# Cutting a 64-column half block of matmuls into 32-column tiles, next to a stage that already uses them

## The chip, the cores and the metric

The kernel runs on one core of one Trainium2 chip. The metric is the device time of one execution in microseconds (us). A run also has a span, from its first to its last instruction, which is about 1.2 us shorter here. Engines are named as in the profile: PE is the matrix engine (TensorE), PEld its weight loads, ACT is ScalarE, DVE is VectorE, POOL is GpSimd. The granted clock is the share of the full PE clock that the run was given, 1.0 for all of it. "The chain that ended last" is the work followed back from the last instruction, at each step to what released it. L585 means line 585 of the kernel. The change adds two lines, so L585, L661, L674 and L787 of the kernel before are L587, L663, L676 and L789 of the kernel after, and lines move similarly in the experiments.

## The reference, cut to what matters

```python
xn = _layernorm(x)                    # 2048 tokens x 640
s  = _A_ref(xn, wqkv, wo)             # linear attention, 32 heads of 20
h  = max(xn @ w1, 0)                  # w1 is 640 x 1728
g  = silu(h @ w2)                     # w2 is 1728 x 640
return x + s * g
```

The width 1728 is 13 blocks of 128 columns and one half block of 64. The change is about the half block of `xn @ w1`.

## The kernel before

Each full block of `w1` is handled by `H_block`: five matmuls (640 = 5 x 128) of a 128 x 128 stationary operand against 512 tokens, accumulated in one bank of PSUM, the memory that PE writes its sums to. For the half block a 128 x 128 pass would leave half of the array's columns empty. So `H_half` pairs two groups of 512 tokens: one group (u = 0) goes to PSUM partitions 0 to 63, the other (u = 1) to 64 to 127, and the two alternate.

```python
def H_half(jp):
    b = nextb()
    fns = []
    ...
    for k in range(C):                       # C = 5
        for u in range(2):
            src = hsrc(2 * jp + u)[0]
            fns.append(lambda eng, k=k, u=u, src=src: eng.matmul(
                ps[b][64 * u:64 * (u + 1), :], lhsT=w1_sb[:, k, NF * P:FF], rhs=src[:, k, :],
                start=(k == 0), stop=(k == C - 1)))
    a = sc.group("PE", fns, R=[("w1", 2)] + keys, W=[("ps", b)])
    ...   # ACT: relu of the whole bank into hTl
```

The attention's denominators are computed right after it, with 32 columns (one for each head) and four groups of 512 tokens side by side, each at a stated position in the array:

```python
def den():
    ...
    for c in range(C):
        for i in range(J):                   # J = 4
            fns.append(lambda eng, c=c, i=i: eng.matmul(
                ps[b][H * i:H * (i + 1), :], lhsT=zmat[:, c, :], rhs=pqT[:, c, schunk(i)],
                start=(c == 0), stop=(c == C - 1), tile_position=(0, H * i)))
    sc.group("PE", fns, R=[("zmat",)] + [...], W=[("ps", b)])
```

The place of both, late in the first half of the kernel:

```python
if n == 9:
    z_col()                                  # 10 one-column matmuls, L661; DVE makes zmat of them
if n == 11:                                  # after the seventh full block of the last 512 tokens
    lastW1 = H_half(0)
    lastW1 = H_half(1)
    den()
```

The counter n runs over a list that mixes full blocks with other work, so 11 is not a count of full blocks. The six full blocks that are left and then the Gram matmuls (L787, the next stage) follow on PE.

Of the kernel before, what the change touches and what calls it, by code (L numbers as in the profile page):

```python
# [208 lines left out]
def bass_recurrent_scan__linear_attn_block__dense_activation_relu__prompt_kernel(  # L209
# [13 lines left out]
    FF = B_w1.shape[1]  # L223
    P = 128
    T = S // P
    J = S // 512
    C = D // P
    NF = FF // P
# [35 lines left out]
    w1_sb = reg5[:, 0:C * FF].rearrange("p (c n) -> p c n", c=C)  # L264
# [43 lines left out]
    ps = [psT[:, 512 * i:512 * (i + 1)] for i in range(8)]  # L308
# [226 lines left out]
    def nextb():  # L535
        b = RB[ring[0] % len(RB)]
        ring[0] += 1
        return b
# [21 lines left out]
    def hsrc(j):  # L560
        if j == 0:
            return xcT[:, :, :], [("xcT", q, h) for q in range(4) for h in range(2)]
        return xnT[:, :, schunk(j)], [("xnT", 4 * j + q) for q in range(4)]
# [12 lines left out]
# [3 lines that stand above are left out]
        keys = []  # L579
        for u in range(2):  # L580
            keys += hsrc(2 * jp + u)[1]
        for k in range(C):
            for u in range(2):
                src = hsrc(2 * jp + u)[0]
                fns.append(lambda eng, k=k, u=u, src=src: eng.matmul(  # L585
                    ps[b][64 * u:64 * (u + 1), :], lhsT=w1_sb[:, k, NF * P:FF], rhs=src[:, k, :],
                    start=(k == 0), stop=(k == C - 1)))  # L587
        a = sc.group("PE", fns, R=[("w1", 2)] + keys, W=[("ps", b)])
        sc.op("ACT", lambda eng: eng.activation(out=hTl[:, jp, :], in_=ps[b], func=ACTF.Relu),
              R=[("ps", b)], W=[("hTl", jp)])  # L590
        return a
# [129 lines left out]
    for j in range(J):  # L721
        for n, item in enumerate(plans[j]):
# [38 lines left out]
            if j == J - 1:  # L761
                while zpend:
                    z_add()
                if n == 1:
                    z_split()
                if n == 9:
                    z_col()
                if n == 11:
# [3 lines that stand above are left out]
# [232 lines left out]
```

## Time and profile before

| | |
|---|---|
| time | 221.32 us, median of 3 runs (221.1 to 221.34) |
| span of the profiled run | 219.3 us, granted clock 1.0 |
| PE busy | 214.8 us, 98% |
| PE's share of the chain that ended last | 94% |
| half block, L585, in the chain | 20 matmuls, 2.28 us, 1.0% |
| denominators, L674, in the chain | 20 matmuls, 1.19 us, 0.5% |

First the busy table of the kernel before, by engine:

```profile
PE 214.8 (98%) x1431; PEld 133.6 (61%) x1441; DVE 119.0 (54%) x219; ACT 84.2 (38%) x140; POOL 43.7 (20%) x69
```

Then the chain of work that ended last, over the stretch in question (start, length, what). A matmul's piece in this view runs from the end of the one before it to its own end, so pieces add up without overlap. "issue" is time in which the engine waited for nothing that the profile shows.

```profile
98.18 0.23 PE psT L661 x10
98.41 2.18 PE psT L568 x10
100.59 2.28 PE psT L585 x20
102.87 1.19 PE psT L674 x20
104.06 0.16 issue
104.22 6.42 PE psT L568 x29
110.64 21.73 PE psT L787 x160
```

The reader should see that PE works without a break and that twenty half block matmuls take 2.28 us, 114 ns each, while ten full ones (L568) take 2.18 us, 218 ns each. A full one streams the same 512 columns. Only two at a time can do that. The timeline of PE shows the pairs (start, length, line, operands in partitions x columns, count):

```profile
98.27 2.32 PE L568 MATMUL psT<-reg 128*128 128x512 bf16 x10
100.52 0.40 PE L585 MATMUL psT<-regX,reg 128*64 128x512 bf16 x1
100.52 0.40 PE L585 MATMUL psT<-reg 128*64 128x512 bf16 x1
100.76 0.38 PE L585 MATMUL psT<-regX,reg 128*64 128x512 bf16 x1
100.76 0.38 PE L585 MATMUL psT<-reg 128*64 128x512 bf16 x1
...
102.80 1.26 PE L674 MATMUL psT<-pqT,zmat 128*32 128x512 bf16 x20
```

A matmul's length of 0.38 us here is longer than the step to the next one: lengths overlap, and the profiler models their ends. What counts for throughput is the step from start to start. The records behind this view have starts to the nanosecond: within a pair 3 to 4 ns, from pair to pair 215 to 216 ns (241 for the first), and among the denominators 2 to 4 ns within a group of four and 216 ns from group to group (226 for the first). I call such a group that starts together a pass. The half block is ten passes, the denominators five.

### The profile page before, as it was taken

To read this page: it belongs to the slowest core of one execution; us is meant where nothing else is said; L and a number is where in the kernel's file an instruction comes from. 1 tells how busy PE (TensorE), PEld (TensorE's weight loads), DVE (VectorE), ACT (ScalarE), POOL (GpSimd) and SP (SyncE) were. 2 spreads that over 40 slices of the span, in tenths; PEclk is the share of its full clock that TensorE was granted. 3 is DMA by queue.
4 is the path that set the end of the run, shared out by engine and by line. 5 is a ranking of instruction groups with operands and counts; after the bars stand their busy time and mean duration, and the time that the engine had idled before them with its cause. 6 is when DMAs were issued, how large, how long until landed. Compare 5 with 4: busy or idle time off the path is not lost.

```text
span 219.3 us, 3503 instructions
## 1 busy us (share of the span) xinstructions
PE 214.8 (98%) x1431; PEld 133.6 (61%) x1441; DVE 119.0 (54%) x219; ACT 84.2 (38%) x140; POOL 43.7 (20%) x69
## 2 busy tenths in 40 slices
PE   8999999999999999999999999999999999999995
PEld 7655554555545555444467777677767776777674
DVE  3789957779639999783702116930424240403134
ACT  5597675666655676554420000551021102110211
POOL 2178501120041699950000000000000000000001
DMA  6977496711001243000099969942110100001011
GB/s 205 368 234 161 110 302 59 199 30 30 3 1 38 51 107 106 0 0 3 3 209 303 374 215 341 373 132 64 38 52 33 60 30 30 33 30 61 3 60 60
DMA packets 28421, 24.72 MB, mean 113 GB/s; under 512 B 12021, under 2 KB 27765, under 8 KB 28405
## 3 DMA queue, kind: packets, MB, share of 16 engines
q1 hardware_dynamic: 24677, 19.77, 32.1%
q10 hardware_dynamic: 3728, 4.73, 6.4%
q8 instruction: 11, 0.18, 0.4%
q14 instruction: 5, 0.04, 0.1%
HBM read 15.81 MB, written 5.24 MB: 96 GB/s over the span
## 4 chain that ended last, share of the span: by engine, by line
PE 94%; DMA 2%; ACT 1%; DVE 1%; issue 0%; DVEq 0%
PE psT L847 26%; PE psT L568 25%; PE psT L787 10%; PE psT L546 10%; PE psT L493 9%; PE psT L898 9%; DMA reg<-in_A_x_dram 2%; PE psT L865 1%; PE psT L585 1%; PE psT L817 1%; PE psT L802 1%; PE psT L674 1%; DVE reg L886 0%; ACT regE L447 0%; PE psT L468 0%
## 5 line engine op out<-in xcount | busy, mean ns | idle before, releaser
L847 PE MATMUL psT<-reg,hT 128*128 128x320 bf16 x416 | 60.5, 299 | 0.0
L847 PEld LDWEIGHTS psT<-reg,hT 128*128 128x128 bf16 x416 | 40.2, 98 | 16.5 <-issue 1.1
L568 PE MATMUL psT<-reg 128*128 128x512 bf16 x192 | 45.5, 379 | 0.3 <-issue 0.2
L886 DVE TENSOR_TENSOR reg<-psT,reg 128x640 bf16<-128x640 f32 (+2 forms) x18 | 13.3, 749 | 48.3 <-PE psT L898 47.0
L572 ACT ACTIVATE hT<-psT 128x512 bf16<-128x512 f32 x52 | 30.8, 602 | 18.1 <-PE psT L568 18.1
L568 PEld LDWEIGHTS psT<-reg 128*128 128x128 bf16 x195 | 18.9, 98 | 21.9 <-issue 0.4
L875 ACT ACTIVATE reg<-psT 128x640 bf16<-128x640 f32 x12 | 8.2, 701 | 44.7 <-PE psT L847 25.3
L891 POOL TENSOR_TENSOR reg<-reg 128x224 bf16<-128x224 bf16 x1 | 0.6, 607 | 120.4 <-DVE reg L886 120.4
L898 PE MATMUL psT<-reg,pqT 128*128 128x320 bf16 (+2 forms) x165 | 24.4, 295 | 0.0
L504 POOL TENSOR_TENSOR zacc<-zacc,reg 128x640 f32<-128x640 f32 x16 | 23.8, 1487 | 2.3 <-DVE reg L528 1.3
L546 PE MATMUL psT<-reg 128*128 128x512 bf16 x95 | 23.8, 379 | 0.3
L787 PE MATMUL psT<-reg 128*128 128x320 bf16 x160 | 21.9, 299 | 0.0
L898 PEld LDWEIGHTS psT<-reg,pqT 128*128 128x128 bf16 x165 | 16.0, 98 | 5.8
L787 PEld LDWEIGHTS psT<-reg 128*128 128x128 bf16 x160 | 15.6, 98 | 6.3
L510 ACT ACTIVATE regE<-psT 128x640 bf16<-128x640 f32 x24 | 15.6, 701 | 9.1 <-PE psT L493 9.1
L493 PE MATMUL psT<-reg 128*128 128x320 bf16 x120 | 18.3, 299 | 0.0
L554 DVE TENSOR_SCALAR regE<-psT 128x512 bf16<-128x512 f32 x20 | 13.6, 679 | 8.2 <-ACT regE L553 8.2
L556 DVE SCALAR_TENSOR_TENSOR pqT<-regE 128x512 bf16<-128x512 bf16 x20 | 17.3, 867 | 0.7
L546 PEld LDWEIGHTS psT<-reg 128*128 128x128 bf16 x100 | 9.8, 98 | 11.7
L493 PEld LDWEIGHTS psT<-reg 128*128 128x128 bf16 x120 | 11.7, 98 | 6.5 <-DMA reg<-reg 0.2
L792 DVE CAST reg<-psT 128x640 bf16<-128x640 f32 x5 | 4.1, 825 | 20.9 <-PE psT L787 20.9
L553 ACT ACTIVATE regE<-psT 128x512 bf16<-128x512 f32 x20 | 11.9, 597 | 8.8 <-PE psT L546 8.8
(69 smaller groups left out, 177.6 us busy)
## 6 DMA issues: line engine op xcount, KB each, us to landing
scr<-regE SPq DMA_DIRECT2D x4, 640.0 KB, 11.1
reg<-in_A_x_dram SPq DMA_DIRECT2D x4, 640.0 KB, 9.9
out_dram<-reg SPq DMA_DIRECT2D x15, 160.0 KB, 1.8
reg<-in_A_x_dram SPq DMA_DIRECT2D x13, 160.0 KB, 3.2
regE<-scr SPq DMA_DIRECT2D x4, 512.0 KB, 5.3
reg<-in_B_w_dram ACTq DMA_DIRECT2D x1, 1120.0 KB, 12.2
reg<-in_B_w_dram ACTq DMA_DIRECT2D x1, 1040.0 KB, 6.2
reg<-in_A_wo_dram SPq DMA_DIRECT2D x6, 160.0 KB, 3.6
```

The lines of the kernel that those rows point to most:

```text
L493: fns.append(lambda eng, a=a, k=k, lhs=lhs: eng.matmul(ps[b + a][:, 0:HN], lhsT=lhs[:, k, tok(t)], rhs=wqk[:, k, D + HN * a:D + HN * (a + 1)],
L504: sc.op("POOL", lambda eng: eng.tensor_tensor(out=zacc[:, :], in0=zacc[:, :], in1=pk[:, t, :], op=ALU.add), R=[("zacc",), ("pk", t)], W=[( ...
L510: sc.op("ACT", lambda eng: eng.activation(out=o_.rearrange("p (a n) -> p a n", a=2), in_=ps2(b, HN), func=func, scale=scale), R=[("ps", b) ...
L546: sc.group("PE", [(lambda eng, k=k: eng.matmul(ps[b], lhsT=wqk[:, k, P * f:P * (f + 1)], rhs=xnT[:, k, schunk(j)], start=(k == 0), stop=(k ...
L554: sc.op("DVE", lambda eng: eng.tensor_scalar(out=r_, in0=ps[b], scalar1=0.0, scalar2=1e-6, op0=ALU.max, op1=ALU.add), R=[("ps", b), ("er_e ...
L556: sc.op("DVE", lambda eng: eng.scalar_tensor_tensor(out=pqT[:, f, schunk(j)], in0=e_, scalar=1.0, in1=r_, op0=ALU.min, op1=ALU.add), R=[(" ...
L568: a = sc.group("PE", [(lambda eng, k=k: eng.matmul(ps[b], lhsT=w1_sb[:, k, P * f:P * (f + 1)], rhs=src[:, k, :], start=(k == 0), stop=(k = ...
L572: sc.op("ACT", lambda eng: eng.activation(out=hT[:, f, schunk(j)], in_=ps[b], func=ACTF.Relu), R=[("ps", b)], W=[("hT", j, f)])
L787: fns.append(lambda eng, t=t, a=a: eng.matmul(ps[b + a][:, 0:HN], lhsT=xn[:, t, P * k:P * (k + 1)], rhs=pk[:, t, HN * a:HN * (a + 1)], sta ...
L847: sc.group("PE", [(lambda eng, f=f: eng.matmul(ps[b][:, 0:HN], lhsT=hT[:, f, tok(t)], rhs=w2_sb[:, f, HN * n:HN * (n + 1)], start=(f == 0 ...
L886: sc.op("DVE", lambda eng: eng.tensor_tensor(out=tmpo[:, os_, lo:hi].rearrange(shp, a=na), in0=src, in1=g_sb[:, t, lo:hi].rearrange(shp, a ...
L898: sc.group("PE", [(lambda eng, c=c: eng.matmul(ps[b][:, 0:hi - lo], lhsT=pqT[:, c, tok(t)], rhs=wf[:, c, lo:hi], start=(c == 0), stop=(c = ...
```

## The change

The half block should use the tiles of the denominators: two 32-column tiles for each 64-column one, at stated positions. Four tiles then run at a time, and both stages use one tiling of the array.

```diff
         for k in range(C):
             for u in range(2):
                 src = hsrc(2 * jp + u)[0]
-                fns.append(lambda eng, k=k, u=u, src=src: eng.matmul(
-                    ps[b][64 * u:64 * (u + 1), :], lhsT=w1_sb[:, k, NF * P:FF], rhs=src[:, k, :],
-                    start=(k == 0), stop=(k == C - 1)))
+                for q in range(2):
+                    r = 64 * u + 32 * q
+                    fns.append(lambda eng, k=k, src=src, q=q, r=r: eng.matmul(
+                        ps[b][r:r + 32, :], lhsT=w1_sb[:, k, NF * P + 32 * q:NF * P + 32 * (q + 1)],
+                        rhs=src[:, k, :], start=(k == 0), stop=(k == C - 1), tile_position=(0, r)))
```

## The prediction

> **What bounds the kernel now.** TensorE. The busy table gives PE 214.8 us of a 219.3 us span (98%), and the chain that ended last is 94% PE, at a granted clock of 1.0. What is saved on PE near 100 us should show almost in full. But what the change touches is small: in the chain, the half block (L585) is 20 matmuls in 2.28 us (1.0%), followed by the denominators (L674), 20 matmuls in 1.19 us (0.5%).
>
> **What these matmuls cost.** In the timeline the half block's matmuls already run two at a time: members of a pair start 3 to 4 ns apart, and pairs follow each other every 215 to 216 ns, the step of one full 128x128x512 matmul of L568. So the 20 matmuls are 10 passes, not 20. The denominators run four at a time: starts 3 to 4 ns apart, quads every 216 ns. (The Trainium skill, "TensorE: Matmul & The Clock Gate", Part 3, The mechanism, gives about 4 ns between starts of concurrent tiles; this trace agrees.)
>
> **What the change does.** Each 64-column matmul becomes two 32-column ones: a pass has four tiles, not two, of the same 128 columns in all. Passes stay 10; at the denominators' step they still cost 10 x 216 ns. 20 matmuls and 20 weight loads are added (about 97 ns each in L674, against 110 ns in L585, overlapped four wide) and fit within the passes, as L674 does with the same four loads a pass. The second tile of a source reads the same moving data again; four different streams already run at full step in L674, so I expect no cost.
>
> It removes one switch of the array's tiling. Start to start, the step from the last L568 matmul to the first L585 is 309 ns, not 216: 93 ns for the switch. From the last L585 to the first L674 it is again 309 ns; from L674 back to L568, 538 ns. (The skill, "TensorEngine Tiling (Array Packing)", Key Properties: changing the tiling mode drains the TensorE; the trace has these gaps where the mode changes, and none between tiles of one mode.) After the change both stages have one mode, so the middle switch should go: about -0.09 us. The first step inside L585 (241 ns) may become L674's (226 ns): -0.015 us. Entry and exit stay.
>
> **Sum.** About -0.1 us, all on the critical path: ACT's evictions of the half block (0.60 us each) are not waited for. That is 0.05%, less than the spread of the three runs (0.24 us). I predict 221.2 us, 8 times in 10 within 220.6 to 221.7; faster by over 2% 0.5%, within 2% 98.5%, slower by over 2% 1%.
>
> **What would show it.** Right: L585 has 40 matmuls 128x32 in groups of four, 3 to 4 ns apart, groups every 216 ns; the step from the last L585 to the first L674 is about 216 ns; the two stages take 3.37 us rather than 3.47 us; later stages start about 0.1 us earlier. Wrong: groups of four step by more than 216 ns (same data read twice, or eight instructions a pass too many), or two of the four run after the other two: up to 2.2 us longer, 223.4 us, still only 1%. Or 309 ns stays before L674: then it is not the switch, but the denominators' own start, such as their weights (zmat, ready near 100.5 us, 2.3 us before use).
>
> **What would make it wrong.** Four-wide tiles serialising, or a difference between chips larger than the effect.

## The result, and the profile after

The kernel after took 221.01 us (median of 6 runs, 220.31 to 221.62); the kernel before, in all its runs up to then, 221.33 us (median of 6, 221.03 to 221.84). The ratio of after to before is 0.9979, with a 95% interval of 0.9955 to 1.0002. Ratios here are the mean time of one kernel's fast runs over that of the other's fast runs of the same rounds, so they are not quite the ratio of the medians.

The difference of 0.12 us that the trace shows is too small for these runs to tell from zero: their interval reaches from 1.0 us faster to slightly slower. So the finding rests on the traces. The chain of the kernel after:

```profile
98.32 0.23 PE psT L663 x10
98.55 2.18 PE psT L568 x10
100.73 2.27 PE psT L587 x40
103.00 1.08 PE psT L676 x20
104.08 0.16 issue
104.24 6.42 PE psT L568 x29
110.66 21.73 PE psT L789 x160
```

Its PE timeline:

```profile
100.66 0.39 PE L587 MATMUL psT<-regX,reg 128*32 128x512 bf16 x2
100.66 0.39 PE L587 MATMUL psT<-reg 128*32 128x512 bf16 x2
100.88 0.38 PE L587 MATMUL psT<-regX,reg 128*32 128x512 bf16 x2
...
102.82 1.25 PE L676 MATMUL psT<-pqT,zmat 128*32 128x512 bf16 x20
```

Forty matmuls take as long as the twenty did (2.27 us against 2.28 us). The denominators' piece is 0.11 us shorter (1.08 against 1.19). Between the start of the piece of the column matmuls (L661, L663) and that of the Gram matmuls (L787, L789) the chain has 110.64 - 98.18 = 12.46 us before and 110.66 - 98.32 = 12.34 us after: 0.12 us saved. I use this distance below as the measure of the stretch, taken from the nanosecond starts (12.462 and 12.342 us). It is free of what happens earlier. Later nothing changes either: from the first Gram matmul to the last matmul of the program it is 105.988 us in both traces, and 105.987 to 105.989 us in the traces of all nine experiments.

And yet both spans are 219.3 us, because the column matmuls started 0.14 us later in the profiled run of the kernel after. That lies before the changed matmuls and is taken up under "Where the noise comes from" below.

### The profile page after: what moved, and what is told of

Same layout as the page of the kernel before. It is cut to its first block, busy times and chain, and to the rows that moved or that the text cites. A ratio compares the mean times of both kernels' runs of the same rounds, so it can differ in the third digit from the quotient of the medians.

```text
span 219.3 us, 3543 instructions
## 1 busy us (share of the span) xinstructions
PE 214.5 (98%) x1451; PEld 133.7 (61%) x1461; DVE 119.1 (54%) x219; ACT 84.2 (38%) x140; POOL 43.8 (20%) x69
## 4 chain that ended last, share of the span: by engine, by line
PE 95%; DMA 2%; DVE 1%; issue 0%; SPq 0%; ACT 0%; DVEq 0%
PE psT L849 26%; PE psT L568 25%; PE psT L493 10%; PE psT L789 10%; PE psT L546 10%; PE psT L900 9%; DMA reg<-in_A_wqkv_dram 2%; PE psT L867 1%; PE psT L587 1%; PE psT L819 1%; PE psT L804 1%; PE psT L676 0%; DVE reg L888 0%; ACT reg L877 0%; PE psT L468 0%
## 5 line engine op out<-in xcount | busy, mean ns | idle before, releaser
L568 PE MATMUL psT<-reg 128*128 128x512 bf16 x192 | 45.5, 379 | 0.3 <-issue 0.2
L568 PEld LDWEIGHTS psT<-reg 128*128 128x128 bf16 x195 | 18.9, 98 | 21.8 <-issue 0.4
L789 PE MATMUL psT<-reg 128*128 128x320 bf16 x160 | 21.9, 299 | 0.0
L789 PEld LDWEIGHTS psT<-reg 128*128 128x128 bf16 x160 | 15.7, 98 | 6.2
L413 DVE BATCH_NORM_STATS2 stats<-reg 128x6 f32<-128x320 bf16 x32 | 14.1, 475 | 2.3 <-DMA reg<-in_A_x_dram 2.3
```

The source lines that it names most:

```text
L413: sc.op("DVE", lambda eng: eng.bn_stats(stats[:, t, a, :], xv[:, HN * a:HN * (a + 1)]), R=[("xin", t % XR)], W=[("stats", t, a)])
L568: a = sc.group("PE", [(lambda eng, k=k: eng.matmul(ps[b], lhsT=w1_sb[:, k, P * f:P * (f + 1)], rhs=src[:, k, :], start=(k == 0), stop=(k = ...
L789: fns.append(lambda eng, t=t, a=a: eng.matmul(ps[b + a][:, 0:HN], lhsT=xn[:, t, P * k:P * (k + 1)], rhs=pk[:, t, HN * a:HN * (a + 1)], sta ...
```

## The experiments

The theory, as the prediction has it (switch theory): what the change saves is one change of the array's tiling, between the half block and the denominators. The rivals: the 32-column tiles are better in themselves (width theory: shorter weight loads, a better pace); the gap before the denominators was their own start, for example a wait for their weights `zmat` (start theory); and the 64-column tiles had not run side by side at all, or only in part.

Marks: the column below headed "stretch" is the distance from the first column matmul to the first Gram matmul in the trace. "Changes" counts the changes of tiling inside it: full to 64 columns, 64 to 32, and so on.

| kernel | changes | passes, half block + denominators | stretch, us | median, us | ratio to before, 95% interval |
|---|---|---|---|---|---|
| before | 3 | 10 + 5 | 12.462 | | |
| after | 2 | 10 + 5 | 12.342 | 221.01 | 0.9979 (0.9955 to 1.0002) |
| mix64 | 12 | 10 + 5 | 13.548 | 221.69 | 1.0034 (1.0011 to 1.0057) |
| mix32 | 2 | 10 + 5 | 12.369 | 221.17 | 1.0007 (0.9986 to 1.0027) |
| sep64 | 4 | 10 + 5 | 12.568 | 220.93 | 1.0017 (0.9981 to 1.0053) |
| sep32 | 4 | 10 + 5 | 12.561 | 221.09 | 1.0005 (0.9982 to 1.0028) |
| split64 | 4 | 10 + 5 | 12.583 | 221.34 | 1.0025 (1.0007 to 1.0043) |
| serial64 | 3 | 11 + 5 | 12.706 | 221.40 | 1.0024 (1.0005 to 1.0042) |
| solo64 | 5 | 20 + 5 | 14.839 | 223.85 | 1.0101 (1.0042 to 1.0160) |
| far64 | 3 | 16 + 5 | 13.783 | 222.45 | 1.0028 (0.9979 to 1.0076) |
| serial32 | 2 | 18 in all | 13.026 | 221.81 | 1.0000 (0.9944 to 1.0057) |

All nine experiments gave correct results. They ran in three calls, each with its own runs of the kernel before (medians 221.01, 220.77 and 221.41 us), so compare a kernel with its own ratio, and kernels with one another by the stretch.

### mix64 and mix32: many changes of tiling, or none

The denominators' five passes go between the ten passes of the half block, as one group of matmuls, so that each of the five has a half block pass on either side.

```diff
+        h = [H_half(jp) for jp in range(2)]      # now only returns its bank, matmuls and keys
+        w = len(h[0][1]) // C
+        order = []
+        for c in range(C):
+            order += h[0][1][w * c:w * (c + 1)] + fns[J * c:J * (c + 1)] + h[1][1][w * c:w * (c + 1)]
-        sc.group("PE", fns, ...)
+        a = sc.group("PE", order, ...)           # and ACT's two evictions after it
```

> The five passes of the denominators are put between the ten two-wide passes of the half block (pair, quad, pair, and so on), the half block still in 64-column tiles: ten changes of tiling inside the stretch instead of one. If each change of tiling costs about 95 to 120 ns (switch theory), the stretch from the last full matmul before to the first after is about 0.9 to 1.1 us longer than in the kernel before, and so is the run (about 0.4 to 0.5%). If the gain of the change came from the 32-column tiles' own pace or lighter loads (width theory), or from the start of the denominators alone, such as their weights (start theory), the stretch stays within 0.1 us of that of before.

> The same interleaving with the half block in 32-column tiles, so that no pass changes the tiling. Switch theory: every pass follows the last after 216 ns, the stretch is as long as in the kernel after (3.89 us start to start), and the run is about 1.0 us faster than mix64. Width and start theories: only about 0.1 us between mix64 and mix32.

The chain of mix64 (L585 is the half block in 64 columns, L675 the denominators), its first passes and its end:

```profile
101.83 0.36 PE psT L585 x2
102.20 0.33 PE psT L675 x4
102.53 0.55 PE psT L585 x4
103.08 0.33 PE psT L675 x4
...
106.06 0.34 PE psT L585 x2
106.39 6.58 PE psT L568 x30
```

The same part of mix32 (L587 and L677):

```profile
100.79 0.36 PE psT L587 x4
101.15 0.21 PE psT L677 x4
101.36 0.43 PE psT L587 x8
101.80 0.22 PE psT L677 x4
...
103.95 0.22 PE psT L587 x4
104.17 6.58 PE psT L568 x30
```

A pass of the denominators costs 0.33 us where its neighbours have another tiling, and 0.21 to 0.22 us, its streaming time, where they have the same. The whole difference is 13.548 - 12.369 = 1.179 us for ten changes of tiling, 118 ns for each; against the kernel before mix64 is 1.086 us longer, where 0.9 to 1.1 was expected. mix64's changes lie inside one group of matmuls, within which the trace has no semaphore wait, so the gaps are not waits at the border of two stages. Nothing else differs between mix64 and mix32 but the width of the half block's tiles, and the kernels before and after show what that alone does when there is one change between them: 0.120 us.

Both mixes have a first pass of 0.36 us, since there the whole group waits for `zmat`: DVE finishes it at 100.694 us in mix32 and the first matmul starts at 100.749 us, 336 ns after the last full one and not 309. That accounts for the 0.03 us by which mix32 is longer than after.

On the clock the two differ less than in the trace: the ratios are 1.0034 and 1.0007, 0.27% or about 0.6 us of 221, where the trace has 1.18 us (0.53%). The two intervals are each 0.2% wide to a side and allow both values. mix64 is the one of the two that is clearly slower than the kernel before.

### sep64 and sep32: the same number of changes with both widths

The half block moves ahead of the seventh full block. Each stage then has full matmuls on both sides, and nothing is shared.

```diff
-                if n == 11:
+                if n == 10:
                     lastW1 = H_half(0)
                     lastW1 = H_half(1)
+                if n == 11:
                     den()
```

> Half block (64 columns) one full block ahead of the denominators, so both have full 128-column matmuls on either side: four changes of tiling instead of three. Switch theory: about 0.1 us longer than before, and equal to sep32 within 0.03 us. Width theory: 0.1 us slower than sep32.

> The same with 32-column tiles: four changes of tiling instead of the two of the kernel after. Switch theory: about 0.2 us longer than after, the change's gain is gone, half block equal to sep64's within 0.03 us. Width theory: keeps 0.1 us against sep64.

The half block in the chain of sep64:

```profile
100.03 2.28 PE psT L585 x20
```

And in that of sep32:

```profile
100.84 2.27 PE psT L587 x40
```

The stretches are 12.568 and 12.561 us, 7 ns apart. 32-column tiles give no gain of their own, so the width theory falls. sep64 has one change more than before and is 0.106 us longer; sep32 has two more than after and is 0.219 us longer, by which the gain is gone and more. The clock cannot rank these two (both intervals include 1).

sep64 also settles a wait that the profile suggests. In the kernel before it puts 0.42 us of idle time of PEld ahead of the half block down to DVE's `zmat`, which ends 21 ns before the first of these matmuls. In sep64 the half block starts at 99.964 us, 1.05 us before `zmat` is done (101.016), and the step into it is still 310 ns. So the gap at the entry does not need that wait.

### split64: do the denominators cause the gap?

Half block, denominators, half block, all as before in width.

```diff
                     lastW1 = H_half(0)
-                    lastW1 = H_half(1)
                     den()
+                    lastW1 = H_half(1)
```

> Order: half block of the first two sources (64 columns), denominators (32 columns), half block of the other two (64 columns). Switch theory: four changes of tiling, each with a step of about 309 ns, also from the denominators back to 64 columns; stretch about 0.1 us longer than before. Start theory (the gap of before belongs to the denominators' start, their weights or their wait): the step into the second half block, which waits for nothing new, is 216 ns, and the stretch is as long as before.

The timeline of PE in split64:

```profile
102.32 0.38 PE L585 MATMUL psT<-reg 128*64 128x512 bf16 x1
102.63 1.26 PE L674 MATMUL psT<-pqT,zmat 128*32 128x512 bf16 x20
103.82 1.27 PE L585 MATMUL psT<-reg 128*64 128x512 bf16 x10
```

The step from the last denominator matmul (record at 103.510 us) to the first matmul of the second half block (103.819 us) is 309 ns, the same as the step into the denominators. These half block matmuls have no new wait, and the same gap. The stretch is 0.121 us longer than before, for one change more. The start theory falls. (On the clock split64 is 0.07 to 0.43% slower than before, where the trace has 0.055%; four runs with the start-up noise shown below are not a finer measure than that.)

A first form of this test, with the denominators ahead of both half blocks, was not run: the denominators' later data overwrite a buffer that the first half block still reads.

### serial64: did the pairs of before really run side by side?

The two loops of `H_half` are exchanged: five matmuls into the left 64-column tile, then five into the right one.

```diff
-        for k in range(C):
-            for u in range(2):
+        for u in range(2):
+            for k in range(C):
```

> The half block of before with the order turned: all five passes of one source, then all five of the other, so that two neighbours in the queue write the same 64-column tile and cannot run side by side. If the pairs of before already ran side by side, this takes 20 steps of 216 ns, not 10: about 2.16 us longer (1.0%). If 64-column tiles without a stated tile position had been running one after the other anyway (a rival reading, under which the change had up to 1 to 2 us to win), the time stays as before.

Neither number came: the stretch is 0.244 us longer than before, just over one pass of 216 ns. In the timeline (matmuls that read regX are those of the left tile, for the first pair of sources):

```profile
101.33 0.62 PE L585 MATMUL psT<-regX,reg 128*64 128x512 bf16 x2
101.57 0.40 PE L585 MATMUL psT<-reg 128*64 128x512 bf16 x1
101.78 0.38 PE L585 MATMUL psT<-regX,reg 128*64 128x512 bf16 x1
101.81 0.38 PE L585 MATMUL psT<-reg 128*64 128x512 bf16 x1
```

The program has all five regX matmuls first. In the records the sixth of the program starts at 101.571 us, 5 ns after the second (101.566), and ahead of the third (101.781). So by the records PE did not keep program order between the two tiles; it ran each tile's own row in order, the right tile one pass late, and most of the expected loss was not there. In the passes that follow, the matmul of the right tile is four matmuls later in the program than the left one it runs beside, in eight of nine pairs (in the other, where the second group of matmuls begins, it is one earlier). That suggested a look-ahead of about four matmuls, and with it three more tests.

### solo64, far64, serial32: how far does PE look ahead, and what would no overlap cost?

In solo64 all ten matmuls of the left tile run first, then one full block, then all ten of the right tile. In far64 the two rows of ten are adjacent. serial32 is the kernel after with the order turned.

```diff
# solo64; far64 has both calls under n == 11
+                if n == 10:
+                    H_tile(0)                    # u = 0 for both pairs of sources
                 if n == 11:
-                    lastW1 = H_half(0)
-                    lastW1 = H_half(1)
+                    lastW1 = H_tile(1)           # u = 1 for both, then ACT's evictions
                     den()
# serial32
-        for k in range(C):
-            for u in range(2):
-                ...
-                for q in range(2):
+        for u in range(2):
+            for q in range(2):
+                for k in range(C):
```

> All ten passes of the left 64-column tile (first of each pair of sources), one full block, then all ten of the right tile: nothing of the other tile is near, so no two can run side by side. If the pairs of before run side by side, this takes 20 steps of 216 ns and one more stay in full mode (two switches, about 0.22 us): 2.4 us longer than before from the last full matmul to the Gram matmuls (14.8 us from the first zmat column matmul to the first Gram matmul, where before has 12.46 us), about 1.1% of the run. If 64-column tiles never overlapped, no more than 0.25 us longer.

> The same two rows of ten, next to each other. Strict program order: 20 steps but for one overlap, about 2.0 us longer than before (14.4 us between the two marks). A short look-ahead, as serial64 suggests (there each tile ran four matmuls ahead of program order): the right tile starts when the seventh of the left one starts, 16 steps, about 1.3 us longer (13.8 us). A look-ahead over all ten, limited by the issue of some 20 instructions alone: about 0.5 us longer (13.0 us).

> The kernel after with the order turned: five passes of one 32-column tile, then five of the next. Strict program order: up to 40 steps, over 5 us longer than after. Look-ahead of about four matmuls: each tile starts one step after the one before it and they then run four wide, so 13 steps rather than 10, about 0.65 us longer than after (13.0 us between the marks, where after has 12.34 us).

The chain of solo64 (L587 is the half block, ten matmuls at a time):

```profile
100.79 2.27 PE psT L587 x10
103.06 1.19 PE psT L568 x5
104.25 2.27 PE psT L587 x10
106.53 1.19 PE psT L678 x20
```

Ten matmuls of a single 64-column tile take 2.27 us. In the kernel before twenty of them, in two tiles, took 2.28 us. The stretch is 2.377 us longer than before: ten passes of 216 ns more (2.16 us), and two changes of tiling more (0.22 us). This is what packing was worth, and the kernel before had already earned it. A further doubling of the number of tiles had no empty columns left to fill.

far64 fits the short look-ahead: the stretch is 13.783 us (13.8 was expected for it, 14.4 for strict order, 13.0 for a look-ahead over all ten; the text does not say where its 0.5 us come from, but twenty starts 25 ns apart, as among the column matmuls here, would give it). The right tile's first matmul starts at 102.624 us, 6 ns after the left tile's seventh (102.618), four matmuls later in the program than that one. (Which tile a record belongs to is inferred there: a first matmul of a tile after a change takes 403 ns in the records, the others 379, and the second 403 is this one.) serial32 fits as well: 13.026 us, against 13.0 expected for a look-ahead and more than 5 us of loss under strict order. But it shows that the look-ahead is not four matmuls in all: the fourth tile's first matmul starts at 101.855 us, while six that come earlier in the program are still to start, among them three that read regX (102.034, 102.050 and 102.266). What the three traces have in common is that a tile's first matmul starts when three matmuls of the tile before it are still waiting. Whether that is the rule was not tested. serial32 even lets the next stage in. Its timeline, with L587 the half block and L676 the denominators, which come later in the program:

```profile
103.33 0.38 PE L676 MATMUL psT<-pqT,zmat 128*32 128x512 bf16 x1
103.34 0.41 PE L587 MATMUL psT<-reg 128*32 128x512 bf16 x3
103.55 0.40 PE L676 MATMUL psT<-pqT,zmat 128*32 128x512 bf16 x2
103.58 0.39 PE L587 MATMUL psT<-reg 128*32 128x512 bf16 x2
```

Denominators in tiles that are already free run beside the last half block matmuls, in one tiling. On the clock solo64 is slower than before by 1.0% (0.4 to 1.6%), which agrees; far64 and serial32 lie inside the noise.

None of the experiments pointed to an order with fewer changes of tiling or fewer passes than the kernel after. What is left around this stretch is the entry from full matmuls and the exit to them.

## Why the prediction was right, and where it was loose

**The size.** Predicted: 221.2 us, within 220.6 to 221.7, within 2% with 98.5%. Measured: 221.01 us. The saving predicted was "about -0.1 us"; the trace shows 0.120 us, and the two stages take 3.35 us in the chain (3.37 predicted). The clock adds no support: its median fell by 0.32 us, mostly noise by the trace, and the predicted range holds the 221.33 us of the kernel before as well. That 221.01 lies so near to 221.2 is in part luck.

**Passes stay 10.** Right. 40 matmuls of 128x32, four at a time, 3 to 5 ns apart in a group, 216 ns from group to group; 2.27 us where there were 2.28 us. Reading the same moving data twice cost nothing that shows. Solo64 shows the counterpart: without pairs the same work takes 2 x 2.27 us.

**The middle switch goes.** Right. From the last half block matmul to the first denominator matmul the step was 309 ns; it is 205 ns now. From first of one pass to first of the next (which is the fair measure) it went from 313 to 216 ns, 97 ns less. mix64, sep64, sep32 and split64 show that the gap goes with the change of tiling, in whichever direction and whatever the stage.

**The small first steps.** Right in kind. The first step within a stage after a change is longer too: 241 ns in 64 columns, 226 ns in 32 columns, against 216 ns. The change took away 15 ns of this in the half block (241 to 226), as predicted, and 10 ns in the denominators (226 to 216), which the prediction had left out. 97 + 15 + 10 = 122 ns, against 120 measured.

**All on the critical path.** Right: the later stages are the same to 2 ns in all eleven traces.

**A misread number.** The prediction gave the step from L674 back to L568 as 538 ns, as if that were the price of the change back to full matmuls. It is not: by all signs one matmul record is missing there. The chain of the kernel before has "issue" of 0.16 us and then 29 L568 matmuls in 6.42 us before the Gram matmuls, though the program has six blocks of five there. In mix64 and solo64 the same stretch is complete. The piece of solo64:

```profile
107.72 6.58 PE psT L568 x30
```

30 matmuls in 6.58 us, which is 0.16 + 6.42. In the traces that kept this record the step is 312 ns to the first full matmul and 226 ns to the second, which add up to the 538 ns. The cost of the exit is thus like that of the others, about 0.1 us. The prediction did not use the number, so nothing else fell with it. The sign to look for was at hand: 260 weight loads but 255 matmuls of L568.

**Where the noise comes from.** The prediction named run-to-run differences only as a spread. The traces show the main place. The chain's early pieces in the kernel before and in sep32, the two ends of the range:

```profile
1.46 5.10 DMA reg<-in_A_x_dram
...
12.87 1.24 PE psT L568 x5
```

```profile
1.45 6.44 DMA reg<-in_A_x_dram
...
14.15 0.86 PE psT L568 x4
```

The first load of `x` takes 5.10 us in one and 6.44 us in the other, 1.34 us more, and the column matmuls start at 98.02 us in one and 99.35 us in the other, 1.33 us later. From there on everything is repeatable to a few nanoseconds: from the first full matmul to the column matmuls it is 85.37 us in all eleven traces, once 0.216 us is added in the four that lack the record of its first matmul. So a change worth 0.12 us in the middle of this kernel can be read from one trace, and cannot be seen on the clock with six runs. In the kernel after, the chain begins with a load of `wqkv` instead (5.11 us), and its column matmuls start at 98.15 us; so both profiled spans came to 219.3 us. Why these loads vary was not looked into. There is a second source that no trace shows: three runs (one of sep64, one of solo64, one of the kernel before) had a granted clock of 0.992 and took 1.3 to 2.0 us more than the medians of their kernels, which widens the intervals in these places.

**What stays open.** What the 93 to 97 ns of a change of tiling consist of. The Trainium skill, "TensorEngine Tiling (Array Packing)", Key Properties, says that changing the tiling mode drains the TensorE, and the gaps stand just where the mode changes. But a weight load takes 92 to 111 ns here, and the next weights are not loaded during the last pass before a change (PEld is idle for 0.42 us there, as against 0.12 us between full matmuls). By the records the first load of the new tiling starts 308 ns after the last matmul of the old one and only 1 ns ahead of its own matmul (102.798 and 102.799 us in the kernel before). So the gap lies ahead of that load, which speaks for the drain and against an exposed load. But no run here tests whether a record's start is where the work itself starts, and none separates the two.

## What to carry to other kernels

Count passes, not matmuls: tiles pay by filling empty columns, and when two 64-column tiles already run side by side, four 32-column ones do the same work in the same time. What can still be saved is the change of tiling, here about 0.11 to 0.12 us each time, so put stages of one tiling next to each other and never alternate two of them. When the expected gain is smaller than the spread of the runs, look for a stretch between two marks in the trace that repeats to a few nanoseconds, and measure there; and before you price a gap on PE, count the matmuls against the weight loads, since a lost record looks like a wait.

## What the Trainium skill lacked or had wrong

- "TensorE: Matmul & The Clock Gate", Part 3, The mechanism, under "What overlaps and what doesn't": it says that matmuls start and end in strict program order, without reordering. Here matmuls of different column tiles started out of program order by the records: the sixth of the program 210 ns before the third (serial64), the eleventh 6 ns after the seventh and before the eighth (far64), and denominators before half block matmuls issued ahead of them (serial32). The times of the stretches fit that and not strict order (13.026 us in serial32, where strict order would by estimate cost about 5 us more than 12.342). A tile's first matmul started when three of the tile before it were still waiting (serial64, far64, serial32), with up to six waiting in all (serial32). The section's other statement, that tiles overlap, agrees (3 to 5 ns between starts in the kernel after, where it has about 4).
- The same page says that a single semaphore increment on the last matmul of a group is safe because of that order. No run here breaks it, and all results were correct, but with the order not kept across tiles it deserves its own test.
- "TensorEngine Tiling (Array Packing)", Key Properties: it says that a change of tiling mode drains the engine, and gives no price. Here 93 to 97 ns for the step itself, and with the slower first step after it 106 to 121 ns a change (118 on average over ten).
- "TensorEngine Tiling (Array Packing)", Theoretical Speedup: it gives up to 2x for 64 columns and up to 4x for 32. The 2x was met (10 matmuls in one tile 2.27 us, 20 in two tiles 2.28 us). It doesn't say that cutting 64 columns into 32 adds nothing once the 128 columns are full (40 in four tiles 2.27 us).
